# Loading K and V of one middle head through the first eight DMA engines

## The chip, the cores and the metric

The kernel runs on one core of one Trainium2 chip. The metric is device microseconds of one execution.

Two views are used besides the page of the profile. The trace holds one record for each DMA packet (start, duration, size, queue) and one for each completion: every load of 128 partitions has sixteen of them, as many as the page counts DMA engines, and one is read here as one engine's share that has landed. Neither carries the number of the DMA engine. All times of records are given in microseconds from the start of the span.

## The reference

One decode step of four sequences: a layer norm, then attention over a cached K and V of 32 heads and 8192 keys, and a gated feed-forward block, both added to the input. Cut to what matters here:

```
q = (layernorm(x) @ wq)                       # 4 sequences x 32 heads x 128
p = softmax(q . k_cache / sqrt(128))          # k_cache: 4 x 32 x 8192 x 128, bf16
o = p . v_cache                               # v_cache: the same shape
out = x + o @ wo + ffn(layernorm(x))
```

A pair of sequence and head has 2 MB of K and 2 MB of V. There are 128 pairs ("heads" below, numbered m = 0 to 127), so 537 of the 551 MB that the kernel reads are K and V, each used once. Softmax and the sum over keys don't depend on the order of the keys, as long as K and V have the same one.

## The kernel before

K and V of a head are each loaded by one transfer: partition p takes 64 successive keys, 16 KB of successive bytes. Nine slots of 16 KB per partition hold the tiles in flight.

```python
slots = ctx.enter_context(tc.tile_pool(name="slots", bufs=NSLOT))   # NSLOT = 9

def load_k(m):
    h, b = divmod(m, B)
    t_ = slot()
    nc.sync.dma_start(out=t_[:], in_=A_k_cache[b, h, :, :].rearrange("(p t) d -> p (t d)", p=P))
    k_tiles[m] = t_[:].rearrange("p (t d) -> p t d", d=Dh)

def load_v(m, parts=1):
    h, b = divmod(m, B)
    t_ = slot()
    src = A_v_cache[b, h, :, :].rearrange("(p t) d -> p (t d)", p=P)
    w = SLOT // parts
    for i in range(parts):
        nc.sync.dma_start(out=t_[:, i * w:(i + 1) * w], in_=src[:, i * w:(i + 1) * w])
    v_tiles[m] = t_[:].rearrange("p (t d) -> p t d", d=Dh)

# ... layer norm, q, ffn and wo loads left out ...

for i in range(M + LAGV + 1):                 # M = 128, LAGV = 2
    if i + 2 < M:
        load_k(i + 2)
    if i < M:
        load_v(i, parts=4 if i == M - 1 else 1)
    # ...
    for g in range(NGR):                      # 8 groups of 8 blocks of 128 keys
        if i < M:
            t_group(i, g)                     # transpose K of head i on TensorE, copy to SBUF
        # ... scores of head i, softmax of head i-1 ...
        mp = i - LAGV
        if 0 <= mp < M:
            pv_group(mp, g)                   # o += p . V of head i-2
    # ...
```

All loads are issued by SP, in order, so K(i+2) and V(i) sit beside each other in the queues. The landings are posted on eight completion counters (eight semaphores in the trace), which the transfers take in turn, and a transfer is issued only when the one before it on the same counter, eight transfers before, has landed: in the trace no issue comes less than 0.015 us after that landing.

Of the kernel before, what the change touches and what calls it, by code (L numbers as in the profile page):

```python
# [15 lines left out]
def kernel(  # L16
# [13 lines left out]
    nc = tc.nc  # L30
    P = nc.NUM_PARTITIONS
# [8 lines left out]
    M = B * H  # L40
# [3 lines left out]
    SLOT = T * Dh  # L44
    NSLOT = 9
    LAGV = 2
    LAGS = 2
    NW = 64
    NPB = 4
# [21 lines left out]
    def slot():  # L71
        return slots.tile([P, SLOT], dt.bfloat16, name="slot")
# [6 lines left out]
    for c2 in range(0, EC, 2):  # L79
        t_ = slot()  # L80
# [2 lines left out]

    k_tiles, v_tiles = {}, {}

    def load_k(m):
        h, b = divmod(m, B)
        t_ = slot()
        nc.sync.dma_start(out=t_[:], in_=A_k_cache[b, h, :, :].rearrange("(p t) d -> p (t d)", p=P))  # L89
        k_tiles[m] = t_[:].rearrange("p (t d) -> p t d", d=Dh)  # L90

    def load_v(m, parts=1):
        h, b = divmod(m, B)
        t_ = slot()
        src = A_v_cache[b, h, :, :].rearrange("(p t) d -> p (t d)", p=P)
        w = SLOT // parts
        for i in range(parts):
            nc.sync.dma_start(out=t_[:, i * w:(i + 1) * w], in_=src[:, i * w:(i + 1) * w])  # L98
        v_tiles[m] = t_[:].rearrange("p (t d) -> p t d", d=Dh)

    load_k(0)
    load_k(1)


# [54 lines left out]
    def load_ffn():  # L159
        wg_t, wu_t, wd_t = slot(), slot(), slot()  # L160
        w = EC * F
        nc.sync.dma_start(out=wg_t[:, 0:w], in_=B_w_gate.rearrange("(p c) f -> p (c f)", c=EC))
        nc.sync.dma_start(out=wu_t[:, 0:w], in_=B_w_up.rearrange("(p c) f -> p (c f)", c=EC))
        nc.sync.dma_start(out=wd_t[:, 0:FC * D], in_=B_w_down.rearrange("(p c) e -> p (c e)", c=FC))
        ffn["w"] = (wg_t[:, 0:w].rearrange("p (c f) -> p c f", c=EC),
                    wu_t[:, 0:w].rearrange("p (c f) -> p c f", c=EC),
                    wd_t[:, 0:FC * D].rearrange("p (c e) -> p c e", c=FC))

    def do_ffn():
        wg, wu, wd = ffn["w"]  # L170

        gu_ps = psT.tile([P, 2, FC * B], dt.float32, name="tps")
        for i, w in enumerate((wg, wu)):
            for fc in range(FC):
                for c in range(EC):
                    mm(gu_ps[:, i, fc * B:(fc + 1) * B], w[:, c, fc:F:FC], xnt[:, c, :],
                       start=(i == 0 and fc == 0 and c == 0))
        eg = persist.tile([P, FC * B], dt.float32, name="eg")
        nc.scalar.activation(out=eg[:], in_=gu_ps[:, 0, :], func=ACT.Exp, scale=-1.0)
        nc.vector.tensor_scalar(out=eg[:], in0=eg[:], scalar1=1.0, scalar2=None, op0=ALU.add)  # L180
        sig = persist.tile([P, FC * B], dt.float32, name="sig")
        nc.vector.reciprocal(out=sig[:], in_=eg[:])  # L182
        gs = persist.tile([P, FC * B], dt.float32, name="gs")
        nc.vector.tensor_tensor(out=gs[:], in0=gu_ps[:, 0, :], in1=sig[:], op=ALU.mult)
        ht = persist.tile([P, FC * B], dt.bfloat16, name="ht")
        nc.vector.tensor_tensor(out=ht[:], in0=gs[:], in1=gu_ps[:, 1, :], op=ALU.mult)  # L186
        yf_ps = psT.tile([B, D], dt.float32, name="tps")
        for fc in range(FC):
            mm(yf_ps[0:B, :], ht[:, fc * B:(fc + 1) * B], wd[:, fc, :], start=(fc == 0))
        nc.vector.tensor_tensor(out=yfx[:], in0=yf_ps[0:B, :], in1=xf[:], op=ALU.add)  # L190

    def load_wo(part, nparts):
        n = H // nparts
        h0 = part * n
        nc.sync.dma_start(out=wo_sb[:, h0:h0 + n, :],
                          in_=A_wo[h0 * P:(h0 + n) * P, :].rearrange("(h p) e -> p h e", p=P))
# [5 lines left out]
    def t_group(m, g):  # L202
        tps = psT.tile([P, GT, P], dt.bfloat16, name="tps")
        for u in range(GT):
            nc.tensor.transpose(tps[:, u, :], k_tiles[m][:, g * GT + u, :], ident[:, :])  # L205
        kt = kt_pool.tile([P, GT, P], dt.bfloat16, name="kt")
        if on_dve[g]:
            nc.vector.tensor_copy(out=kt[:], in_=tps[:])  # L208
        else:
            nc.scalar.copy(out=kt[:], in_=tps[:])  # L210
        kts[m, g] = kt
# [6 lines left out]
    def s_group(m, g):  # L218
        if g == 0:
            s_ps[m] = psS.tile([P, 512], dt.float32, name="sps")  # L220
        kt = kts.pop((m, g))
        for u in range(GT):
            t = g * GT + u
            mm(s_ps[m][:, t:t + NW], kt[:, u, :], qt[:, m:m + NW], start=True)

    def max_1(m):
        mx = small.tile([P, 1], dt.float32, name="mx")
        nc.vector.reduce_max(out=mx[:], in_=s_ps[m][:, 0:T], axis=AX.X)  # L228
        sc[m] = mx

    def max_2(m):

        nc.tensor.matmul(s_ps[m][:, C_MX:C_MX + P], lhsT=sc.pop(m)[:, 0:1].to_broadcast([P, P]), rhs=ident_f[:, :],  # L233
                         is_transpose=True, start=True, stop=True, skip_group_check=True)
        nm = small.tile([P, 1], dt.float32, name="nm")
        nc.vector.tensor_reduce(out=nm[:], in_=s_ps[m][:, C_MX:C_MX + P], axis=AX.X, op=ALU.max, negate=True)  # L236
        nb = small.tile([P, 1], dt.float32, name="nb")
        nc.vector.tensor_scalar(out=nb[:], in0=nm[:], scalar1=qscale, scalar2=None, op0=ALU.mult)  # L238
        sc[m] = nb

    def max_3(m):
        p_ = p_buf[m % NPB]
        nc.scalar.activation(out=p_[:, 0:T], in_=s_ps[m][:, 0:T], func=ACT.Exp, bias=sc.pop(m)[:, 0:1], scale=qscale,  # L243
                             accum_out=rs[:, m:m + 1])
        p_sb[m] = p_

    def row_sums(m):
        h = m // B
        mm(s_ps[m][:, C_RS:C_RS + B], ones_f[:, :], rs[:, h * B:(h + 1) * B], start=True)
        rcp = small.tile([P, B], dt.float32, name="rcp")  # L250
        nc.vector.reciprocal(out=rcp[:], in_=s_ps[m][:, C_RS:C_RS + B])  # L251
        sc["rcp", h] = rcp

    def pv_group(m, g):
        h, b = divmod(m, B)
        if g == 0 and b == 0:
            o_ps[h] = psO.tile([P, B, NW], dt.float32, name="ops")
        for u in range(GT):
            t = g * GT + u
            mm(o_ps[h][:, b, :], v_tiles[m][:, t, :], p_sb[m][:, t:t + NW], start=(b == 0 and t == 0))  # L260
# [3 lines left out]
    def fin_1(h):  # L264
        otn = small.tile([P, B], dt.bfloat16, name="otn")
        nc.vector.tensor_tensor(out=otn[:], in0=o_ps.pop(h)[:, :, 0], in1=sc.pop(("rcp", h))[:], op=ALU.mult)  # L266
        sc["otn", h] = otn

    def fin_2(h):
        mm(yo_ps[0:B, :], sc.pop(("otn", h))[:, :], wo_sb[:, h, :], start=(h == 0))  # L270

    for i in range(M + LAGV + 1):

        if i + 2 < M:
            load_k(i + 2)
        if i < M:
            load_v(i, parts=4 if i == M - 1 else 1)
        if i == 1:
            load_ffn()
        if i == 4:  # L280
            do_ffn()
        if 3 <= i < 7:
            load_wo(i - 3, 4)
        for g in range(NGR):
            if i < M:
                t_group(i, g)
            ms = i if g >= LAGS else i - 1
            if 0 <= ms < M:
                s_group(ms, (g - LAGS) % NGR)
            mp = i - LAGV  # L290
            if 0 <= mp < M:
                pv_group(mp, g)
            mx = i - 1
            if 0 <= mx < M:
                if g == LAGS:
                    max_1(mx)
                if g == LAGS + 1:
                    max_2(mx)
                if g == LAGS + 3:
                    max_3(mx)  # L300
                if g == LAGS + 5 and mx % B == B - 1:
                    row_sums(mx)
            mf = i - LAGV - 1
            if 0 <= mf < M and mf % B == B - 1:
                if g == 0:
                    fin_1(mf // B)
                if g == 1:
                    fin_2(mf // B)
# [34 lines left out]
```

## Time and profile before

| | before |
|---|---|
| median time | 1326.1 us |
| HBM read | 550.8 MB, 416 GB/s over the span |
| PE busy | 82% |
| DMA share of the chain of waits | 79% |

The page of the kernel before. In the slices each digit is the busy share of a fortieth of the span in tenths; the queue lines give packets, MB and the time of their packets as a share of 16 engines' span; the last line is the chain that ended last, by engine.

```profile
PE   5876878887788888887887888888887798798787
...
DMA  9999999999999999999999999999999999999994
GB/s 394 428 415 416 428 428 427 428 428 427 428 429 428 427 428 429 427 427 429 428 427 426 431 425 428 428 428 419 418 427 428 421 417 420 430 414 427 422 416 178
...
q1 hardware_dynamic: 42192, 550.79, 98.2%
q8 instruction: 196, 3.21, 0.9%
...
DMA 79%; PE 19%; issue 0%; SPq 0%; DVE 0%; ACT 0%; ACTq 0%; DVEq 0%
```

The engines of the DMA are busy all the time, mostly at 415 to 430 GB/s, up to the last slice. PE is not: the list of waits of the kernel before (who waited for whom: us in total, times, longest) shows what for.

```profile
PE ops L68 <- DMA slot<-in_A_v_cache_dram: 209.9, 114, 4.1
...
PE tps L205 <- DMA slot<-in_A_k_cache_dram: 2.5, 3, 1.3
```

SP, too, waits at times for an earlier load to land, which is the wait on the completion counters; its own list of the kernel before has two lines for K. L98 issues the loads of V, L89 those of K:

```profile
SPq L98 <- DMA slot<-in_A_k_cache_dram: 7.6, 2, 4.6
...
SPq L89 <- DMA slot<-in_A_k_cache_dram: 5.7, 1, 5.7
```

The records add what no average shows. Nearly every 16 KB packet of K or V takes 611 ns, one every 607 ns on an engine (the leading engines take 38.9 us for eight loads of eight packets each). There are also instruction fetches (queue q8, 196 packets of 16 KB, 880 to 1070 ns each, one every 6.7 us), and a data packet beside one mostly takes 1080 to 1160 ns instead of 611. So each fetch costs its engine about 1.4 us (an estimate: some 0.93 us of its own and 0.5 us of the packet beside it). The fetches go to eight of the sixteen engines in turn: from one load to the next most completions come 4.9 us later, but in one group of eight mostly one engine each time comes some 6.3 us later, until all eight have had their turn. So these eight fall behind: they take 40.0 us for eight loads where the others take 38.9. These are the completions of one transfer near the middle, the load of head 64's K, sorted by time:

```
654.8 654.9 654.9 655.1 655.2 656.1 656.5 659.7 | 672.3 672.3 672.3 672.3 672.4 672.4 672.5 672.6
```

Eight engines are done at 655 to 660, the other eight at 672. At the start all sixteen are within 0.6 us; from about 1000 us on the gap stays at some 23 to 25 us. That the nine slots let the leaders run no further is our reading. In the chain PE goes on only after the last completion of a load: the V that was issued at 614.70 us had eight completions by 635.4 us and the last at 648.3, and PE went on at 648.39. So the late eight set the time.

### The profile page before, as it was taken

The numbers are of one execution on the slowest core, as the hardware profiler recorded it, in microseconds if no ns is written. First come the engines' busy times: TensorE is split into PE (matmuls) and PEld (weight loads), VectorE is DVE, ScalarE is ACT, GpSimd is POOL, SyncE is SP. The second block draws the span as 40 slices with busy tenths as digits, with TensorE's granted clock in tenths as the row PEclk, the third lists the DMA queues.
The fourth block names the chain that finished last, engine by engine and source line by source line (L and its number), as shares of the span: only waits on it lengthen the run. The fifth ranks groups of instructions, "written<-read, shape, count | busy, mean of one in ns | idle before, by whom it ended". The sixth has DMA issues, their size and how long they took to land.

```text
span 1324.9 us, 52903 instructions
## 1 busy us (share of the span) xinstructions
PE 1082.4 (82%) x25058; PEld 1047.0 (79%) x25058; DVE 520.3 (39%) x1107; ACT 431.0 (33%) x644; POOL 1.7 (0%) x12
## 2 busy tenths in 40 slices
PE   5876878887788888887887888888887798798787
PEld 5776878887787888887887887878787788787787
DVE  3233344343343443433433434334343343343443
ACT  2222333333333333333333333333333333333332
POOL 0000000000000000000000000000000000000000
PEclk9789999899999988999999989999999999998999
DMA  9999999999999999999999999999999999999994
GB/s 394 428 415 416 428 428 427 428 428 427 428 429 428 427 428 429 427 427 429 428 427 426 431 425 428 428 428 419 418 427 428 421 417 420 430 414 427 422 416 178
DMA packets 42409, 554.17 MB, mean 418 GB/s; under 512 B 4296, under 2 KB 8400, under 8 KB 8912
## 3 DMA queue, kind: packets, MB, share of 16 engines
q1 hardware_dynamic: 42192, 550.79, 98.2%
q8 instruction: 196, 3.21, 0.9%
q14 instruction: 21, 0.17, 0.0%
HBM read 550.77 MB, written 0.00 MB: 416 GB/s over the span
## 4 chain that ended last, share of the span: by engine, by line
DMA 79%; PE 19%; issue 0%; SPq 0%; DVE 0%; ACT 0%; ACTq 0%; DVEq 0%
DMA slot<-in_A_v_cache_dram 78%; PE tps L205 9%; PE ops L68 5%; PE sps L68 4%; DMA slot<-in_A_k_cache_dram 2%; PE tps L68 1%; PE sps L233 0%; SPq L89 0%; PE yo_ps L68 0%; SPq L81 0%; DVE res L311 0%; DVE sig L182 0%; SPq L98 0%; SPq L76 0%; ACT p_buf L243 0%
## 5 line engine op out<-in xcount | busy, mean ns | idle before, releaser
L208 DVE COPY kt<-tps 128x1024 bf16<-128x1024 bf16 x640 | 442.6, 692 | 765.1 <-PE tps L205 751.4
L210 ACT COPY kt<-tps 128x1024 bf16<-128x1024 bf16 x384 | 388.6, 1012 | 873.9 <-PE tps L205 872.9
L205 PE MATMUL tps<-ident,slot 128*128 128x128 bf16 x8192 | 653.5, 225 | 5.4 <-issue 2.5
L68 PE MATMUL ops<-p_buf,slot 128*128 128x64 bf16 x8192 | 425.5, 196 | 216.2 <-DMA slot<-in_A_v_cache_dram 209.9
L205 PEld LDWEIGHTS <-slot 128*128 128x128 bf16 x8192 | 511.0, 101 | 18.8 <-issue 14.2
L68 PEld LDWEIGHTS <-slot 128*128 128x128 bf16 x8432 | 334.6, 100 | 236.6 <-DMA slot<-in_A_v_cache_dram 225.0
L68 PE MATMUL sps<-qt,kt 128*128 128x64 bf16 x8192 | 429.0, 196 | 2.9 <-issue 1.6
L68 PEld LDWEIGHTS <-kt 128*128 128x128 bf16 x8192 | 358.0, 100 | 4.5 <-issue 3.3
L243 ACT ACTIVATE p_buf<-sps,nb 128x64 bf16<-128x64 f32 x128 | 40.9, 319 | 2.7 <-DVE nb L238 2.7
L233 PE MATMUL sps<-ident_f,mx 128*128 128x128 f32 x128 | 39.1, 306 | 0.1
L236 DVE TENSOR_REDUCE nm<-sps 128x1 f32<-128x128 f32 x128 | 37.3, 292 | 4.1 <-PE sps L233 3.8
L228 DVE TENSOR_REDUCE mx<-sps 128x1 f32<-128x64 f32 x128 | 27.5, 215 | 0.6 <-PE sps L68 0.6
L243 ACT ACTIVATION_READ_ACCUMULATOR p_buf<-sps,nb 128x1 f32 x128 | 25.9, 203 | 0.0
L238 DVE TENSOR_SCALAR nb<-nm 128x1 f32<-128x1 f32 x128 | 19.7, 154 | 4.4
L233 PEld LDWEIGHTS sps<-ident_f,mx 128*128 128x128 f32 x128 | 17.8, 139 | 0.6 <-DVE kt L208 0.4
L68 PE MATMUL tps<-xnt,slot 128*128 128x4 bf16 x240 | 10.6, 182 | 6.4 <-DMA slot<-in_A_wq_dram 6.4
L68 PE MATMUL yo_ps<-wo_sb,otn 128*4 128x512 bf16 x32 | 14.5, 454 | 0.3 <-DVE otn L266 0.3
L68 PE MATMUL sps<-rs,ones_f 128*128 128x4 f32 x64 | 11.6, 252 | 0.1
L68 PEld LDWEIGHTS sps<-rs,ones_f 128*128 128x128 f32 x64 | 9.6, 190 | 0.2 <-ACT p_buf L243 0.2
L68 PE MATMUL tps<-slot,ht 128*4 128x512 bf16 x14 | 5.2, 550 | 1.6 <-DVE ht L186 1.6
L251 DVE RECIPROCAL rcp<-sps 128x4 f32<-128x4 f32 x32 | 5.8, 181 | 1.0 <-PE sps L68 1.0
L140 PE MATMUL tps<-ident,kt 4*128 4x4 bf16 x4 | 0.3, 172 | 6.6 <-DVE kt L135 6.6
(36 smaller groups left out, 21.2 us busy)
## 6 DMA issues: line engine op xcount, KB each, us to landing
slot<-in_A_k_cache_dram SPq DMA_DIRECT2D x128, 2048.0 KB, 37.6
slot<-in_A_v_cache_dram SPq DMA_DIRECT2D x127, 2048.0 KB, 33.4
slot<-in_A_wq_dram SPq DMA_DIRECT2D x2, 2048.0 KB, 9.6
wo_sb<-in_A_wo_dram SPq DMA_DIRECT2D x4, 1024.0 KB, 18.8
slot<-in_A_v_cache_dram SPq DMA_DIRECT2D x4, 512.0 KB, 29.9
slot<-in_B_w_gate_dram SPq DMA_DIRECT2D x1, 1792.0 KB, 39.8
slot<-in_B_w_up_dram SPq DMA_DIRECT2D x1, 1792.0 KB, 35.6
slot<-in_B_w_down_dram SPq DMA_DIRECT2D x1, 1792.0 KB, 38.5
```

The source lines that it names most:

```text
L68: nc.tensor.matmul(out_ap, lhsT=lhsT, rhs=rhs, start=start, stop=True, skip_group_check=True, **kw)
L140: nc.tensor.transpose(xnt_ps[:, c, :], xn_bf[0:B, c:D:EC], ident[0:B, 0:B])
L205: nc.tensor.transpose(tps[:, u, :], k_tiles[m][:, g * GT + u, :], ident[:, :])
L208: nc.vector.tensor_copy(out=kt[:], in_=tps[:])
L210: nc.scalar.copy(out=kt[:], in_=tps[:])
L228: nc.vector.reduce_max(out=mx[:], in_=s_ps[m][:, 0:T], axis=AX.X)
L233: nc.tensor.matmul(s_ps[m][:, C_MX:C_MX + P], lhsT=sc.pop(m)[:, 0:1].to_broadcast([P, P]), rhs=ident_f[:, :], is_transpose=True, start=Tru ...
L236: nc.vector.tensor_reduce(out=nm[:], in_=s_ps[m][:, C_MX:C_MX + P], axis=AX.X, op=ALU.max, negate=True)
L238: nc.vector.tensor_scalar(out=nb[:], in0=nm[:], scalar1=qscale, scalar2=None, op0=ALU.mult)
L243: nc.scalar.activation(out=p_[:, 0:T], in_=s_ps[m][:, 0:T], func=ACT.Exp, bias=sc.pop(m)[:, 0:1], scale=qscale, accum_out=rs[:, m:m + 1])
L251: nc.vector.reciprocal(out=rcp[:], in_=s_ps[m][:, C_RS:C_RS + B])
```

## The change

One head in the middle (m = 64) is loaded another way. Each of its two tiles is loaded by four transfers of 32 partitions, and the source rows are presented with an outermost dimension of 8. The rows are taken in another order for this, the same for K and V. The intent, as far as the code tells, is to give work to the first eight engines and to take it from the other eight.

```diff
+    LOW = (M // 2,)
...
+    def transfer(t_, src, parts, low):
+        src = src.rearrange("(p t) d -> p (t d)", p=P)
+        if low:
+            for i in range(0, P, 32):
+                nc.sync.dma_start(out=t_[i:i + 32, :], in_=src[i:i + 32, :].rearrange("(q e) n -> e q n", e=8))
+        else:
+            w = SLOT // parts
+            for i in range(parts):
+                nc.sync.dma_start(out=t_[:, i * w:(i + 1) * w], in_=src[:, i * w:(i + 1) * w])
+
     def load_k(m):
         h, b = divmod(m, B)
         t_ = slot()
-        nc.sync.dma_start(out=t_[:], in_=A_k_cache[b, h, :, :].rearrange("(p t) d -> p (t d)", p=P))
+        transfer(t_, A_k_cache[b, h, :, :], 1, m in LOW)
...
-    def load_v(m, parts=1):
+    def load_v(m):
...
+        transfer(t_, A_v_cache[b, h, :, :], 4 if m == M - 1 else 1, m in LOW)
```

More of the change, by code (lines that the diff above doesn't have):

```diff
@@ L88, in load_k @@
         t_ = slot()
-        nc.sync.dma_start(out=t_[:], in_=A_k_cache[b, h, :, :].rearrange("(p t) d -> p (t d)", p=P))
+        transfer(t_, A_k_cache[b, h, :, :], 1, m in LOW)
         k_tiles[m] = t_[:].rearrange("p (t d) -> p t d", d=Dh)
-    def load_v(m, parts=1):
+    def load_v(m):
         h, b = divmod(m, B)
         t_ = slot()
-        src = A_v_cache[b, h, :, :].rearrange("(p t) d -> p (t d)", p=P)
-        w = SLOT // parts
-        for i in range(parts):
-            nc.sync.dma_start(out=t_[:, i * w:(i + 1) * w], in_=src[:, i * w:(i + 1) * w])
+        transfer(t_, A_v_cache[b, h, :, :], 4 if m == M - 1 else 1, m in LOW)
         v_tiles[m] = t_[:].rearrange("p (t d) -> p t d", d=Dh)
@@ L276 @@
         if i < M:
-            load_v(i, parts=4 if i == M - 1 else 1)
+            load_v(i)
         if i == 1:
```

## The prediction

> **What bounds the kernel now.** The loads. The page's slices show DMA at 9 tenths in 39 of 40 and mostly 415 to 430 GB/s; PE is busy 82% of 1324.9 us. The chain of waits is 79% DMA. The list of waits shows PE waiting 210 us in all for V, at most 4.1 us at a time: compute has 1 to 2 us of slack per head of about 10 us.
>
> The packet records show more. Every K or V packet (16 KB) takes 611 ns. The 16 engines are not alike: 196 instruction packets (930 to 960 ns, one every 6.7 us) go round-robin to eight of them, and the data packet beside one takes some 1080 ns, so each costs its engine about 1.4 us: 34 us per engine over the run. The completion records agree: all 16 within 0.6 us at the start, then eight ahead of the other eight by 16.5 us halfway, 22 us at 800 us, and constant at 24 us after that, where the buffers let them run no further. The slower eight set the time (40.0 us per eight transfers, the others 38.9).
>
> **What the change does.** One head's K and V are 4 MB, 16 packets (9.7 us) per engine. Now the first eight engines carry 32 each (19.5 us), the others none. K and V share the new key order, so the result, PE, ACT and DVE are unchanged. SP issues six more DMAs at 0.33 to 0.47 us; it mostly waits. They share the eight completion counters, so later issues wait for nearer predecessors; queued work (7 transfers, 34 us) should cover that.[...] The trace doesn't number engines.
>
> **Gain or loss.** If the first eight are the leading ones (my guess, 80%: the change makes sense only so), the slower eight are spared 9.7 us of the critical path, and the lead falls by 19.5 us to about -3 us and grows back to some 13 us. Against that: half of the packets go to partitions 64 to 127[...].[...] If the first eight are the slower ones: +9.7 us[...].
>
> **Predicted time: 1324.5 us, 8 in 10 between 1314.5 and 1336.** Faster by over 2%: 1%; within 2%: 98%; slower by over 2%: 1%.
>
> **What will show it.** Completion records: lead near 0 after the middle head, growing again, below 24 us at the end. Packet records: in the two transfers, up to 256 packets of about 1200 ns[...], or all at 611 ns[...]. Mean GB/s near 430 there if nothing is lost. PE, ACT, DVE busy unchanged.
>
> **What would make it wrong.** The instruction packets sit on the first eight engines;[...] the shared counters starve engines around the middle head; the 24 us lead at the end is worth something I don't see (the slower eight keep 39.9 us per eight transfers after it saturates).

The sum came to 1324.5 us, close to the span of the kernel before (1324.9 us). In the likelier branch the 9.7 us that the slower eight are spared, which alone would give about 1316 us, stood against a second term of about the same size for the packets to partitions 64 to 127; in the other branch, 9.7 us more, such a term made it about 18 us. That the transfers take the first eight engines was an assumption of the forecast, too; its grounds are cut, and so is the item of the last paragraph that the second term might be larger than assumed.

## More of the kernel before

Stretches of ten microseconds around the middle of the kernel before. The columns are the stretch, its length, busy time of five engines with counts, granted clock, mean busy share of the 16 DMA engines, and GB/s.

```profile
core 0: us, PE busy (x) PEld busy (x) DVE busy (x) ACT busy (x) POOL busy (x), PEclk, DMA share, GB/s
640.00:650.00 10.00, 9.73 (x221) 9.61 (x219) 4.05 (x9) 4.06 (x6) 0.00 (x0) 0.90 1.00 426
654.00:664.00 10.00, 8.32 (x200) 7.79 (x198) 4.02 (x9) 3.34 (x5) 0.00 (x0) 1.00 1.00 424
678.00:688.00 10.00, 9.22 (x192) 9.21 (x193) 3.42 (x8) 3.34 (x5) 0.00 (x0) 0.83 1.02 434
695.00:705.00 10.00, 7.90 (x191) 7.39 (x188) 4.03 (x9) 2.95 (x6) 0.00 (x0) 1.00 1.01 431
719.00:729.00 10.00, 6.87 (x174) 6.74 (x171) 4.05 (x9) 3.05 (x5) 0.00 (x0) 1.00 1.00 426
```

The last two columns are the baseline to remember: share 1.0 and 424 to 434 GB/s.

## The result, and the profile after

| | before | after |
|---|---|---|
| median time | 1326.1 us | 1358.3 us |
| range of the runs | 1325.9 to 1327.1 | 1357.4 to 1359.4 |
| ratio, 95% interval | | 1.0241, 1.0224 to 1.0259 |

A ratio is the mean time of one kernel's fast runs over that of the other's of the same rounds, so it isn't quite the ratio of the medians. The change costs 32.2 us, and the time lies outside the predicted range.

The page of the changed kernel, the lines that answer to those of before:

```profile
PE   5977878888888888888666788788887888888887
...
DMA  9999999999999999999999999999999999999992
GB/s 395 428 410 421 428 428 427 430 427 428 427 428 429 427 429 426 428 429 427 330 284 359 427 427 425 427 428 418 417 426 425 424 428 410 428 422 428 418 421 98
...
q1 hardware_dynamic: 42224, 550.79, 97.6%
q8 instruction: 195, 3.19, 0.8%
...
DMA 82%; PE 17%; issue 0%; SPq 0%; DVE 0%; ACT 0%; ACTq 0%
```

The bytes are the same. Slices 20 to 22 carry the loss: 330, 284 and 359 GB/s instead of about 428, at a DMA busy share that still reads 9. The engines were busy and slow, not idle. The last slice differs as well (98 GB/s instead of 178), to which we come back.

The waits of PE and of SP in the changed kernel; line numbers have moved, L69 and L215 are the lines L68 and L205 of before. The second block is from SP's list: L93 issues the loads of the middle head, L97 all others of K and V.

```profile
PE ops L69 <- DMA slot<-in_A_v_cache_dram: 218.2, 113, 10.4
...
PE tps L215 <- DMA slot<-in_A_k_cache_dram: 9.7, 4, 5.4
```

```profile
SPq L97 <- DMA slot<-in_A_k_cache_dram: 42.0, 7, 9.9
...
SPq L93 <- DMA slot<-in_A_k_cache_dram: 15.4, 4, 5.7
```

PE now waits up to 10.4 us at once for V and up to 5.4 us for K; these longest waits are in the middle stretch. SP waits longer on the completion counters (42.0 and 15.4 us for K, where it had 7.6 and 5.7), which makes them a suspect.

The chain of waits around the middle, in order of time (start, us, what): first two of the DMA pieces of the kernel before, then three of the changed one in about the same place.

```profile
614.70 33.64 DMA slot<-in_A_v_cache_dram
...
655.09 33.32 DMA slot<-in_A_v_cache_dram
```

```profile
614.54 33.58 DMA slot<-in_A_v_cache_dram
648.14 42.80 DMA slot<-in_A_k_cache_dram
690.96 39.38 DMA slot<-in_A_v_cache_dram
```

A piece is a load from issue to landing. Two consecutive loads, the last of the four small ones of K and of V of the middle head, take 42.8 and 39.4 us instead of 33 to 34, and nothing else lies between them: each was issued within 0.02 us of the landing of the load before it in the chain, which had the same completion counter. That, too, points at the counters.

The same stretches of ten microseconds as before, of the changed kernel:

```profile
640.00:650.00 10.00, 9.80 (x212) 9.67 (x210) 4.14 (x10) 3.66 (x6) 0.00 (x0) 0.86 1.00 424
654.00:664.00 10.00, 5.85 (x108) 5.08 (x106) 1.45 (x3) 2.02 (x2) 0.00 (x0) 0.83 1.05 242
678.00:688.00 10.00, 7.70 (x167) 7.56 (x165) 3.27 (x7) 3.34 (x5) 0.00 (x0) 0.88 1.02 249
695.00:705.00 10.00, 9.50 (x179) 9.50 (x180) 3.04 (x7) 3.34 (x5) 0.00 (x0) 0.70 1.01 228
719.00:729.00 10.00, 1.03 (x28) 0.90 (x24) 1.41 (x3) 0.03 (x1) 0.00 (x0) 0.79 1.04 231
740.00:750.00 10.00, 8.80 (x221) 8.57 (x219) 4.87 (x10) 3.34 (x5) 0.00 (x0) 1.00 1.00 423
```

There are four stretches in which all sixteen engines are busy (share 1.0) and move little more than half of what they moved before. By 740 us everything is back to normal. Over the whole stretch from 640 to 750 us the share is 0.99 (1.01 before) and the rate 331 GB/s (428 before): of 110 us some 25 are lost (an estimate from the rates), of which idle engines can be only some 2 (from the shares). So it is not that engines were left without work. The packet records in the first of the four: all 49 data packets that started from 656 to 660 us took 1225 to 1261 ns. At that pace 49 packets in 4 us are some fifteen engines' work (an estimate: 49 times 1.24 us over 4 us), not that of a few.

The completions say which transfer does it. These are the eight completions (one per engine) of the four small loads of K; the n-th writes partitions 32(n-1) to 32n-1. (Each has a ninth record, 1.1 to 1.2 us after its issue and at least 15 us before the others, which is left out.)

```
partitions   0-31:   652.5 652.5 652.6 653.5 654.2 | 658.5 | 676.7 676.8
partitions  32-63:   654.9 655.0 655.0 656.6 657.9 | 663.4 | 679.1 679.2
partitions  64-95:   659.5 659.5 660.0 661.7 663.0 | 668.5 | 684.5 684.5
partitions  96-127:  664.4 664.5 665.2 666.6 668.1 | 674.5 | 689.4 690.9
```

Two things are to be read here. First, the eight engines are not one group: five are early, one is some 5 us behind, two are some 23 us late. Second, the earliest engine takes 2.4 us from the first to the second load, the normal pace of four packets of 607 ns, and 4.6 and 4.9 us for the third and fourth. The four slow stretches of the table are the times in which the early five (654 to 664, and 695 to 705 for V) and the late two (678 to 688, and 719 to 729 for V) write partitions 64 to 127.

What the late engines lose, from the last completion of a load in both kernels (us):

| load | before | after | difference |
|---|---|---|---|
| V of head 61, issued just ahead of K of head 64 | 667.7 | 677.1 | +9.4 |
| K of head 64 | 672.6 | 690.9 | +18.3 |
| K of head 66, just ahead of V of head 64 | 693.6 | 715.3 | +21.7 |
| V of head 64 | 698.4 | 730.3 | +31.9 |
| K of head 67 | 703.2 | 734.9 | +31.7 |

The loss is complete by the end of V of head 64 and is never made up. It is also not only where the late engines have the head's data themselves: 9.4 us are gone before they reach it.

### The profile page after: what moved, and what is told of

It reads as the page before. It is cut to its first block, busy times and chain, and to the rows that moved or that the text cites. A ratio compares the mean times of both kernels' runs of the same rounds, so it can differ in the third digit from the quotient of the medians.

```text
span 1356.6 us, 52913 instructions
## 1 busy us (share of the span) xinstructions
PE 1095.8 (81%) x25058; PEld 1059.3 (78%) x25058; DVE 520.2 (38%) x1107; ACT 431.0 (32%) x644; POOL 1.7 (0%) x12
## 4 chain that ended last, share of the span: by engine, by line
DMA 82%; PE 17%; issue 0%; SPq 0%; DVE 0%; ACT 0%; ACTq 0%
DMA slot<-in_A_v_cache_dram 76%; PE tps L215 8%; DMA slot<-in_A_k_cache_dram 6%; PE ops L69 5%; PE sps L69 4%; PE sps L243 0%; SPq L97 0%; PE yo_ps L69 0%; SPq L82 0%; DVE res L321 0%; SPq L77 0%; ACT p_buf L253 0%; DVE nm L246 0%; DVE otn L276 0%; DVE nb L248 0%
## 5 line engine op out<-in xcount | busy, mean ns | idle before, releaser
L215 PE MATMUL tps<-ident,slot 128*128 128x128 bf16 x8192 | 659.8, 226 | 14.7 <-DMA slot<-in_A_k_cache_dram 9.7
L69 PE MATMUL ops<-p_buf,slot 128*128 128x64 bf16 x8192 | 429.8, 197 | 222.4 <-DMA slot<-in_A_v_cache_dram 218.2
L215 PEld LDWEIGHTS <-slot 128*128 128x128 bf16 x8192 | 516.7, 102 | 27.7 <-issue 21.0
L69 PEld LDWEIGHTS <-slot 128*128 128x128 bf16 x8432 | 338.4, 101 | 245.1 <-DMA slot<-in_A_v_cache_dram 222.3
L69 PE MATMUL sps<-qt,kt 128*128 128x64 bf16 x8192 | 432.5, 197 | 5.7 <-issue 4.5
L69 PEld LDWEIGHTS <-kt 128*128 128x128 bf16 x8192 | 361.2, 101 | 6.4 <-issue 5.0
L69 PE MATMUL tps<-xnt,slot 128*128 128x4 bf16 x240 | 10.6, 182 | 6.2 <-DMA slot<-in_A_wq_dram 6.2
L69 PE MATMUL yo_ps<-wo_sb,otn 128*4 128x512 bf16 x32 | 14.5, 454 | 0.3 <-DVE otn L276 0.3
L69 PE MATMUL sps<-rs,ones_f 128*128 128x4 f32 x64 | 11.6, 252 | 0.1
L69 PEld LDWEIGHTS sps<-rs,ones_f 128*128 128x128 f32 x64 | 9.6, 190 | 0.2 <-ACT p_buf L253 0.2
L69 PE MATMUL tps<-slot,ht 128*4 128x512 bf16 x14 | 6.1, 622 | 1.6 <-DVE ht L196 1.6
L69 PEld LDWEIGHTS <-ht 128*4 128x4 bf16 x14 | 1.6, 120 | 5.3 <-issue 3.6
```

Source lines behind the costliest of these rows:

```text
L69: nc.tensor.matmul(out_ap, lhsT=lhsT, rhs=rhs, start=start, stop=True, skip_group_check=True, **kw)
L215: nc.tensor.transpose(tps[:, u, :], k_tiles[m][:, g * GT + u, :], ident[:, :])
```

## The experiments

The theory after the traces, theory A, has two parts. Two of the engines that set the time are among the first eight, so they carry more instead of less. And what these eight engines write to partitions 64 to 127 slows the loads, on all engines. Its rivals: transfers on eight engines, or their jumping source rows, are slow wherever they land (B); the additional transfers on the same eight completion counters starve the engines (C); the uneven load of the engines alone is the cost (D); the way from the first eight engines to partitions 64 to 127 is slow by itself (E).

Why the eight engines should do harm at these partitions and not at 0 to 63 is not seen in the trace: a packet's record has neither its engine nor its partition. What the runs can show is which transfers, to which partitions, come with slow packets. In the changed kernel's transfers of 32 partitions, eight engines take four packets each: eight completions for 32 rows, 2.4 us from one load to the next at the normal pace.

### Which engines are late: sixteen tiny loads

The kernel before, with sixteen tiny loads in the second half, the n-th on n engines. Each was to wait behind what its engines have queued, and so it does: within one of these loads the late completions come 17 to 25 us after the early ones, and the sixteen completions of the kernel before are 22 us apart at 793 us.

```diff
+    def probe(k):
+        t_ = persist.tile([16, 32], dt.bfloat16, name=f"probe{k}")
+        nc.sync.dma_start(out=t_[0:k, :], in_=A_wq[0:k, 0:32])
...
+        if i >= 60 and i % 4 == 0 and i < 124:
+            probe((i - 60) // 4 + 1)
```

> Kernel before plus 16 tiny loads (64 bytes per row) in the second half of the run, the n-th on the first n engines. Each rides behind what its engines have queued, so its completion records tell how many of the first n engines are in the late group (17 to 24 us behind). The theory of the prediction, first eight all leading: 0 late up to n=8, then one more per step to 8 at n=16. My theory now, from the changed kernel's records (of the eight completions of a small transfer, five early, one 4 to 6 us later, two 22 us later): 2 late at n=8 and 8 late at n=16. If none of the small transfers of the change landed late for that reason but because of the transfers themselves: 0 late at n=8. Time within 1% of before, result correct.

Measured: 1328.1 us once (before 1326.5 us), result correct. The completions of the loads on 5, 6, 7 and 8 engines, without a first record that came before the others, like the ninth of the changed kernel's small loads:

```
5 engines: 796.1 796.2 797.3 798.5 802.3
6 engines: 835.1 835.1 836.8 837.4 841.1 | 858.2
7 engines: 874.1 874.2 875.7 876.3 880.0 | 898.5 898.6
8 engines: 914.5 914.6 914.7 914.7 915.2 919.9 | 937.4 939.0
```

| engines used | 1 to 5 | 6 | 7 | 8, 9 | 10 | 11 | 12 | 13 | 14 | 15, 16 |
|---|---|---|---|---|---|---|---|---|---|---|
| of them late | 0 | 1 | 2 | 2 | 3 | 4 | 5 | 6 | 7 | 8 |

A step in the lower row names an engine. Counted from 0, in the order in which these loads take them in, the late engines are 5, 6 and 9 to 14. Engine 3 is the one that lags a few us (it appears with the load on four engines: 757.2, 757.3, 759.0, 762.5). So the first eight hold six leaders and two laggards. That each load takes the engines of the load before and one more, and that the change's transfers take the first eight, was assumed. The records agree with it: every load posted as many completions as it had rows, the late ones came in steps of at most one, and the load on eight engines shows the pattern of the changed kernel's small loads (five early, one some 5 us behind, two some 23 to 24 us behind). Engine numbers below are meant in this order.

### The same extra load, to partitions 0 to 63 and to 64 to 127

The kernel before, with four extra transfers in the form of the change's. They write into a part of the wo buffer that is no longer read. Each of the first eight engines carries 16 packets more (9.7 us at 607 ns), and nothing is taken from the others. The two kernels differ in the partitions, 0 to 63 or 64 to 127, and with them in the half of the head whose rows are read. (The exchange of the halves, below, keeps the rows and moves only the destination.)

```diff
+    def extra(i):
+        src = A_k_cache[0, i // 4, :, :].rearrange("(p t) d -> p (t d)", p=P)
+        for j in (0, 32):          # the other kernel: (64, 96)
+            nc.sync.dma_start(out=wo_sb[j:j + 32, 0:16, :].rearrange("p h e -> p (h e)"),
+                              in_=src[j:j + 32, :].rearrange("(q e) n -> e q n", e=8))
...
+        if i in (72, 80):
+            extra(i)
```

Partitions 0 to 63:

> Kernel before plus four extra transfers of 512 KB on the first eight engines, in the form of the change's (same row order, same size), into partitions 0 to 63 of a buffer that is no longer read: 16 packets more per low engine (9.7 us), none for the others. Theory A (what hurts is writing to partitions 64 to 127[...], and two late engines are among the first eight): packets stay at 611 ns, time rises by 9.7 us (8 to 12). Rival B (eight-engine transfers, or their jumping source rows, are slow wherever they land): packets near 1200 ns during them and a rise of 25 us or more. Rival C (more DMAs on the same eight completion counters starve the engines): packets at 611 ns but gaps, and the same rise as in the run with partitions 64 to 127. The prediction's own picture (first eight lead): no rise.

Partitions 64 to 127:

> The same four extra transfers, same rows order, size and number, into partitions 64 to 127. Theory A: packets near 1200 ns while they are written; if only the engine[...] is slowed, time rises by about 19.5 us (9.7 own, 9.7 because own packets go at half rate); if all 16 engines are slowed, as the changed kernel's packets suggest, the late engines lose another 5 us in each of the two stages in which the early ones write, about 29 us. Rivals B and C: the same rise as with partitions 0 to 63.

| | median | ratio to before, 95% interval | more than before |
|---|---|---|---|
| before, same chip | 1326.5 us | | |
| extra to partitions 0-63 | 1334.8 us | 1.0061, 1.0044 to 1.0078 | 8.3 us |
| extra to partitions 64-127 | 1359.7 us | 1.0249, 1.0234 to 1.0264 | 33.2 us |

Stretches in which the early engines write the first two extra transfers: first the kernel with partitions 0 to 63, then the one with 64 to 127.

```profile
756.00:766.00 10.00, 8.68 (x216) 8.48 (x212) 4.20 (x10) 3.34 (x5) 0.00 (x0) 1.00 1.01 428
```

```profile
756.00:766.00 10.00, 7.69 (x155) 7.56 (x152) 3.20 (x7) 2.33 (x4) 0.00 (x0) 0.83 1.03 238
```

428 against 238 GB/s, with the same engines, row order, sizes and number of transfers. From 760 to 768 us all 106 packets of the second kernel took over 900 ns; in the first kernel no stretch of 4 us around the extra transfers (740 to 904 us) has more than three packets over 640 ns, which is the usual number beside instruction fetches. The destination makes a difference of 24.9 us. Rival B falls, as the same transfers are not slow to partitions 0 to 63. Rival C falls as well: both kernels put the same number of transfers on the counters, and SP's waits for K loads, the line that had suggested C, are nearly the same. SP's list, again first the kernel with partitions 0 to 63, then the other:

```profile
SPq L89 <- DMA slot<-in_A_k_cache_dram: 40.0, 9, 6.0
```

```profile
SPq L89 <- DMA slot<-in_A_k_cache_dram: 49.0, 9, 9.8
```

SP waits 40 us there and the kernel loses 8.3; in the next experiment the same line is 33.8 us, and nothing is lost. What was expected for partitions 64 to 127 was about 29 us with all sixteen engines slowed and 19.5 us if fewer were; 33.2 us fit the first, and are 4 us more.

### The extra load on leaders only

The same again, but on four engines, into partitions 0 to 15 and 32 to 47.

```diff
+        for j in (0, 32):
+            nc.sync.dma_start(out=wo_sb[j:j + 16, 0:16, :].rearrange("p h e -> p (h e)"),
+                              in_=src[j:j + 16, :].rearrange("(q e) n -> e q n", e=4))
```

> As the run with extra transfers to partitions 0 to 63 (which cost 8.3 us), but on the first four engines only[...]: the same 16 packets more per engine, now on engines that all lead. Theory A (the 8.3 us came from the late engines 5 and 6 among the first eight): no rise, -2 to +2 us. Rival (any extra data or any eight- or four-engine transfer costs): 4 us or more.

Measured: 1326.9 us, before 1327.2 us on the same chip, ratio 0.9999 (0.9984 to 1.0013), result correct. Sixteen packets more on each of engines 0 to 3 cost nothing. So the 8.3 us of the load on eight engines come from engines 4 to 7, of which 5 and 6 are late, and a leader has room to spare. The prediction's idea of leaders was right for these four.

### K alone

```diff
-        transfer(t_, A_v_cache[b, h, :, :], 4 if m == M - 1 else 1, m in LOW)
+        transfer(t_, A_v_cache[b, h, :, :], 4 if m == M - 1 else 1, False)
```

> The change for K of the middle head only; V is loaded as before, so keys and values of that head are paired wrongly, on purpose (the result may be off). Theory A: half of the cost: 4.9 us own data for engines 5 and 6, 5 to 6 us while the early engines write to partitions 64-127, 5 us while engines 5 and 6 do: 15 to 17 us. If the cost were a single stall around the head (queue emptied once, counters): about as much as the whole change, over 25 us, or nearly nothing.

Measured: 1342.1 us, before 1327.2 us, ratio 1.0116 (1.0101 to 1.0131). The wrong pairing of keys and values of one head is too small to show in the check of the result. The cost is 15 us, a little under half of the whole. Two of the four slow stretches are gone:

```profile
654.00:664.00 10.00, 6.69 (x145) 6.16 (x141) 2.40 (x5) 3.03 (x5) 0.00 (x0) 0.91 1.04 238
678.00:688.00 10.00, 8.58 (x164) 8.39 (x162) 3.34 (x7) 3.34 (x5) 0.00 (x0) 0.76 1.02 231
695.00:705.00 10.00, 9.61 (x228) 9.48 (x226) 4.17 (x10) 4.24 (x6) 0.00 (x0) 0.93 1.01 429
719.00:729.00 10.00, 6.90 (x139) 6.77 (x135) 3.04 (x6) 1.91 (x2) 0.00 (x0) 0.83 1.01 429
```

K makes the first and second, V the third and fourth. The cost adds up per transfer; it is not one stall around the head.

### The halves exchanged

The change with the first two blocks sent to partitions 64 to 127 and the last two to 0 to 63.

```diff
-                nc.sync.dma_start(out=t_[i:i + 32, :], in_=src[i:i + 32, :].rearrange("(q e) n -> e q n", e=8))
+                j = (i + 64) % P
+                nc.sync.dma_start(out=t_[j:j + 32, :], in_=src[i:i + 32, :].rearrange("(q e) n -> e q n", e=8))
```

> The change with the four blocks sent to the other half of the partitions: the first two small transfers of K and of V write 64-127, the last two 0-63; same source order, result correct. Theory A: the stretch of 1200 ns packets comes with the first two small transfers instead of the last two (completions of the early engines some 5 us apart for the first two, 2.4 us for the last two); time as with the change, 1354 to 1363 us. If it were the place in the source or in the queue: the slow stretch stays with the last two.

Measured: 1361.5 us once, result correct. The first completions of the four loads of K are 654.0, 658.9, 663.3 and 666.0 us, where the change had 652.5, 654.9, 659.5 and 664.4. The step of 4.9 us is now between the first and the second load and the step of 2.7 between the third and fourth. The slow stretch (most packets over 900 ns) began at 651 us instead of 655. It follows the destination, with the same rows of the source. One step does not fit the expectation: from the second to the third the first engine still needed 4.4 us, not 2.4. It was then writing partitions 0 to 31, which in the pair of extra loads cost no packet time (at most three over 640 ns in 4 us), while other engines, up to 9 us behind it, were still writing 64 to 127 (the completions of the second load went on to 663.1 and 667.8). That again is slowing that reaches an engine which is not writing there itself.

### Small transfers without uneven load

The change's small transfers, but with rows in natural order, so that all sixteen engines should take two rows of each. (Plain loads of 16 rows and of 128 had sixteen completions; those of these small transfers were not counted.)

```diff
-                nc.sync.dma_start(out=t_[i:i + 32, :], in_=src[i:i + 32, :].rearrange("(q e) n -> e q n", e=8))
+                nc.sync.dma_start(out=t_[i:i + 32, :], in_=src[i:i + 32, :])
```

> The same eight small transfers of 32 partitions each, in natural row order, so that all 16 engines take two rows of each: no engine carries more than before[...]. Theory A[...]: packets near 1200 ns in both stages, early and late engines; time up by 15 to 25 us. Rival D (uneven load alone costs[...]): no rise, within 3 us.

Measured: 1359.3 us (1354.0 to 1360.9), before 1327.2 us, ratio 1.0235 (1.0208 to 1.0263), result correct. If the rows are spread like that, no engine carries more than before, and the cost is the same as the change's; rival D falls. From 656 to 658 us no packet took under 640 ns (25 of 26 took 1250 to 1400). The rise is above the expected 15 to 25 us. The completions show part of the reason: at the load that follows V of head 64, seven of the late engines stand at 724.8 to 727.4 us where the late eight of before stood at 701.5 to 703.2 (+24), but one stands at 736.0. Why that one fell 10 us further behind was not found.

### How far the slowing reaches

Eight separate transfers at eight times, on 8, 4 or 2 engines.

```diff
+    STAGES = {70: (8, 0), 78: (8, 64), 86: (4, 64), 94: (2, 64), 102: (1, 64), 110: (1, 0), 116: (1, 96), 122: (2, 32)}
+    def stage(i, k, j):
+        src = A_k_cache[0, i // 4, :, :].rearrange("(p t) d -> p (t d)", p=P)
+        nc.sync.dma_start(out=wo_sb[j:j + 4 * k, 0:16, :].rearrange("p h e -> p (h e)"),
+                          in_=src[j:j + 4 * k, :].rearrange("(q e) n -> e q n", e=k))
```

> Kernel before plus eight separate extra transfers, some 80 us apart, each on the first 8, 4 or 2 engines, four packets or one per engine: eight engines to partitions 0-31, eight to 64-95, four to 64-79, two to 64-71, four (one row each) to 64-67, four to 0-3, four to 96-99, two to 32-39. It asks how far the slowing reaches.[...] If the slowing spreads to all 16 engines, some stages show all packets near 1200 ns[...]. Transfers to partitions 0-63[...]: no slow packets.[...] Time not of interest (about 10 us over before).

With k = 1 the outer dimension of 1 falls away and the transfer runs on four engines with one packet each, as the completion records show. Packets by their duration while the early engines write, in pieces of 4 us (the transfers on eight engines come back later, when engines 5 and 6 reach them):

```
transfer                        piece      packets  over 640 ns  over 900 ns  median
8 engines, part. 0-31           735-745    no piece with more than 3 over 640
8 engines, part. 64-95          820-824    55       55           55           1205
4 engines, part. 64-79          904-908    55       51           49           1302
                                908-912    77       77           18           702
2 engines, part. 64-71          992-996    90       61           9            698
4 engines, one row each, 64-67  1072-1076  98       10           6            611
4 engines, one row each, 0-3    1152-1156  107      4            2            611
```

(The last two transfers, to 96-99 and 32-39, left no piece with more than 6 over 640.) Four engines with 16 packets in all to partitions 64 to 79 are enough to bring nearly every packet, whatever its engine, to some 1300 ns for about 4 us (49 of 55 over 900 ns, and 229 GB/s at a DMA share of 1.03 from 904 to 909 us). With two engines and 8 packets most packets lengthen, at the median by about 15% (698 ns instead of 611). A single row per engine is hardly seen (10 of 98 over 640 ns). With eight and four engines the number of slow packets is far above the number written, and above twice that (32 by the eight, and 86 over 900 ns from 818 to 826 us; 16 by the four, and 67 in the two pieces shown), so the slowing spreads. It depends on how many engines write there at once; in the changed kernel, engine 3, which lags between the two groups, wrote partitions 64 to 127 alone from 708 to 718 us, and then few packets were slow (5 of 46 over 900 ns from 708 to 710).

### The same transfers with nothing beside them

The kernel before; after the output has left, the extra transfers run alone.

```diff
...
+    def low_rows(j):
+        nc.sync.dma_start(out=wo_v[j:j + 32, :], in_=ksrc[j:j + 32, :].rearrange("(q e) n -> e q n", e=8))
...
+    for j in (64, 96):
+        low_rows(j)                       # 8 engines, as in the change
+    for j in (0, 32):
+        low_rows(j)
+    nc.sync.dma_start(out=wo_v[64:128, :], in_=ksrc[64:128, :])     # 64 rows to partitions 64 to 127
+    nc.sync.dma_start(out=wo_v[:, :], in_=ksrc[:, :])               # 128 rows to all partitions
```

> Kernel before with extra transfers after the output has left, when nothing else moves: on the first eight engines 8 packets each to partitions 64-127, then 8 each to 0-63; then one plain transfer of 64 rows to partitions 64-127 on all 16 engines (4 packets each[...]); then one plain transfer of all 128 rows. Theory A[...]: the first two near 611 ns after the first packets, the 64-row transfer near 1200 ns, the last 611 again. Rival E (the path of the first eight engines to partitions 64-127 is slow by itself): the first group near 1200 ns even alone, and the 64-row transfer slow for eight engines only. Time up by about 30 us, of no interest.

Measured (1353.6 us once, result correct). Three stretches of this kernel's profile: eight engines on both halves, the 64 rows to partitions 64 to 127, the 128 rows to all partitions.

```profile
1328.00:1334.00 6.00, 0.00 (x0) 0.00 (x0) 0.00 (x0) 0.00 (x0) 0.00 (x0) 0.50 0.50 213
1337.00:1340.00 3.00, 0.00 (x0) 0.00 (x0) 0.00 (x0) 0.00 (x0) 0.00 (x0) 0.50 0.88 186
1346.00:1349.00 3.00, 0.00 (x0) 0.00 (x0) 0.00 (x0) 0.00 (x0) 0.00 (x0) 0.50 1.01 431
```

Eight engines (share 0.50) move 213 GB/s to partitions 64 to 127, and then to 0 to 63, at 609 to 634 ns a packet in both after the first few; so the way there isn't slow, and rival E falls. With the 64 rows, more engines are busy (a share of 0.88 of sixteen) and move no more into partitions 64 to 127 than the eight did: 186 GB/s, with packets of 942 to 1305 ns, most of them over 1270. So packets to these partitions are slow without any other traffic, too, when more than eight engines write there. Over all partitions the rate is 431 GB/s again, at a share of 1.01.

## Why the prediction was wrong

Point by point:

- "The slower eight set the time", because of the instruction fetches: right. Packets beside fetches, the two groups of eight and the growing lead are all in the traces, and 16 packets more on each of engines 0 to 3 cost nothing.
- "If the first eight are the leading ones (my guess, 80%)": wrong, and so was its other branch. The split isn't by halves. Engines 5 and 6 are late, 0 to 4 and 7 lead. So the step that the slower eight are spared 9.7 us failed: for two of the engines that set the time the change adds 9.7 us instead of sparing 9.7; the extra transfers to partitions 0 to 63 measured that part alone as 8.3 us. The prediction inferred a fact about the chip from the intent of the change.
- "Half of the packets go to partitions 64 to 127": that this is what costs is shown by the pair of extra loads (24.9 us between the two), and that the slow packets follow the destination by the exchange of the halves (from 651 us instead of 655). With nothing beside them, eight engines wrote there at 213 GB/s and more than eight at 186.
- What these packets cost: the term is the mis-sized one, in its reach. They bring the packets of all sixteen engines from 611 to some 1200 to 1300 ns: the prediction allowed up to 256 packets of about 1200 ns, and from 640 to 740 us 565 took over 900 ns (17 in the kernel before). The early engines write to these partitions some 24 us before engines 5 and 6 do, so there are two stages for K and two for V instead of one each, and the engines that set the time lose in all four. Sized at 9.7 us, it measured 24.9 us (33.2 minus 8.3).
- The sum: 8.3 us of own data and 24.9 us for the destination are 33.2 us, from the extra transfers; the change, with as many packets more on engines 5 and 6 and as many to partitions 64 to 127, measured 32.2 us. The branch closest to it, "If the first eight are the slower ones", about +18 us with its term, had the own data right and lacked the spread. It was given too little weight in the range.
- "Completion records: lead near 0 after the middle head, growing again": not so. At 970 us fourteen engines lie within 12 us of each other and two are some 23 us behind the middle of these (995.0). At the end these two alone finish the loads, which is why the last slice moves 98 GB/s instead of 178.
- "The shared counters starve engines": did not decide. SP waited 42 us on loads of K, but it did about as much in the kernel that lost only 8.3 us and in the one that lost nothing (40.0 and 33.8), and around the middle head the sixteen engines were busy 0.99 of the time.
- "PE, ACT, DVE busy unchanged": right but for 13 us more of PE (1095.8 instead of 1082.4 us). Of these, 4.2 us arose before 640 us, where both kernels load alike; the rest was not examined.

Open: by what mechanism the packets to partitions 64 to 127 slow those of all sixteen engines, and why one engine that writes there alone (engine 3) slows so few (5 of 46). Nor was it found why one engine fell 10 us further behind in the run with rows in natural order.

No version that beats the kernel before came out of this. In the loads of 128 partitions nearly every packet takes 611 ns. To take rows from the late engines meant, in the form tried here, that other engines write partitions 64 to 127, and with the packets of one head that cost 24.9 us (in the extra transfers), more than the 9.7 us at stake. Whether a few rows moved by a single engine would pay was not tried.

## What to carry to other kernels

Before shifting work between DMA engines, find out which engines are late: tiny loads on 1, 2, 3, ... engines, whose completions are sorted into early and late, name them; here they cost 1.6 us in the one run. Keep every load on 128 partitions in the form in which packets take their 611 ns here; even 1 MB that eight engines wrote to partitions 64 to 127 nearly halved the rate of all sixteen engines while it lasted (238 instead of 428 GB/s), and this kernel, bound by its loads, never got that back. When a stretch shows a DMA share of 1.0 with half of the usual GB/s (1.05 and 242 here), look at the destinations of the transfers, not at their issue.
